# A retention mixer on one core: an item's split issued ahead of the next item's differences, and another order for the last gates and the last output rows

## The chip, the cores and the metric

One core of one Trainium2 chip runs the whole kernel in one launch. The metric is device time in microseconds (us). The median of 3 runs of the kernel before is 1352.68 (1351.59 to 1354.52). Engines are named as the profile names them: PE is the matrix engine (TensorE), PEld its weight loads, DVE the vector engine, ACT the scalar engine, POOL the GpSimd engine, SP the queue from which the DMAs start.

## The reference

Three layers follow each other, all in float32:

```
attention (8 batches, 8 heads, 576 rows, 64 columns):
    ret = (scale * q @ k.T) * decay(row - column);   x = ret @ v     -> 8 x 576 x 512
mixing:
    u = x + (x.T @ U @ V).T                          U, V of rank 32
    x2 = u + relu(u @ w_ch1) @ w_ch2                 512 -> 2048 -> 512
gated channel:
    xk, xr = mu * x2 + (1 - mu) * (x2 one row earlier)
    k = relu(xk @ w_k);  v = (k * k) @ w_v           512 -> 1024 -> 512
    out = sigmoid(xr @ w_r) * v
```

The rows of all batches together are 4608 columns of the kernel's tiles, which it treats as 9 blocks of 512. A float32 product is made of three matmuls: a value is split into a high part (a cast) and a low part (the value less the cast), and the products high × high, low × high and high × low are added in PSUM.

## The kernel before, in words

The whole kernel is under a manual schedule: each engine runs its instructions in the order in which the program issues them. Several large products are made by a scheme with seven products for a 2 × 2 block product, so that sums and differences of blocks are formed first.

Until 537 us the kernel does the attention, the mixing of low rank and `h = relu(u @ w_ch1)`. Then comes the stage around which the change stands, the second matrix of the mixing layer (`h @ w_ch2`) for blocks 0 to 7. It is cut into 64 **items**, in 4 quarters `q` of two halves `h` with 8 steps `j` each. An item of the first half (h = 0) gives four of the seven products (24 matmuls of 512 columns), one of the second half three (18 matmuls). Four groups of PSUM banks, `a` to `d`, two banks each, gather the products over the 8 steps.

The work of an item is spread over the engines. `load_item` (L464) loads its tiles `ra`, `rb` from memory, issued by SP. `sums_item` (L476) forms two differences on DVE: L480 and L481 in a first half, and SP stores the second of them for use in the second half; L484 and L485 in a second half. `split_item` (L487) makes for `ra` and then `rb` a cast on ACT (L499: `sah`, `sbh`) and a subtraction on DVE (L500: `sal`, `sbl`). `products` (L518) issues the matmuls (L540). At a half's last step `leave_group` (L550) takes the results out of the banks: copies on ACT (L554, L576), and for the products 4 and 3, at the quarter's end, additions on DVE that read banks `c` and `d` (L580). What is left to be done with them is put in a list, `rest`: additions on POOL (L557, L568, L571, L584, L590), an addition on DVE that reads banks `b` (L560), each final one with a small copy on ACT (L515) and a store by SP (L516). `load_rest` (L509) loads the tiles `ur` which they need.

The loop over items (L1372 to L1389) issues in iteration n: the loads of n+4, the differences of n+2, the split of n+1, the products of n, and then up to two entries of `rest`, except in a half's last step.

After the items, block 8 is projected (L620 to L622). Then, for each pair of blocks and last for block 8 alone in two sides of 256 columns, `gates` (L1423) makes the seven products for two column groups `g`, alternating between two sets of banks; `key_group` (L1465) makes the keys; and `value_part` (L1497) gathers the output products in four banks (L1507), multiplies them by the gate on DVE (L1517) and stores them (L1518). The matmuls of gates and keys are both at L1411; `load_keys` (L319) loads the key weights `wk` at L324.

Of the kernel before, what the change touches and what calls it, by code (L numbers as in the profile page):

```python
# [9 lines left out]
F32 = mybir.dt.float32  # L10
# [6 lines left out]
ALU = mybir.AluOpType  # L17
# [11 lines left out]
BT = 512  # L29
NB = T // BT  # L30
L = 64
NL = S // L
KD = DM // 128
# [7 lines left out]
def retention_mixer_kernel(ctx: ExitStack, tc: tile.TileContext, io):  # L41
    nc = tc.nc
# [14 lines left out]
    def unit(pool, dt, nm):  # L57
        return pool.tile([128, 2, 512], dt, tag="unit", name=nm)

    def small(dt, nm):  # L60
        return sm.tile([128, 512], dt, tag="small", name=nm)
# [179 lines left out]
    wv = [Weight(f"wv_{g}", io["moe2_w_v"][g * 512:(g + 1) * 512, :]) for g in range(2)]  # L241
# [5 lines left out]
    NG = DF2 // 256  # L247
# [209 lines left out]
    def col(p):  # L457
        return slice(p * 128, (p + 1) * 128)

    ITEMS = [(q, h, j) for q in range(NB // 2) for h in range(2) for j in range(NF // 2)]  # L460
# [3 lines left out]
    def load_item(n):  # L464
        q, h, j = ITEMS[n]
        ra[n] = unit(big2, F32, f"ra{n}")
        rb[n] = unit(big2, F32, f"rb{n}")
        if h == 0:
            nc.sync.dma_start(ra[n], hp[q][:, j, 0:2])
        else:  # L470
            nc.sync.dma_start(ra[n][:, 0], t1_blk[q][:, j])
        nc.sync.dma_start(rb[n], hp[q][:, j, 2:4])
# [3 lines left out]
    def sums_item(n):  # L476
        q, h, j = ITEMS[n]
        a, b = ra[n], rb[n]
        if h == 0:
            nc.vector.tensor_tensor(b[:, 0], b[:, 0], a[:, 1], op=ALU.subtract)  # L480
            nc.vector.tensor_tensor(a[:, 1], a[:, 1], a[:, 0], op=ALU.subtract)  # L481
            nc.sync.dma_start(t1_blk[q][:, j], a[:, 1])
        else:
            nc.vector.tensor_tensor(a[:, 0], b[:, 0], a[:, 0], op=ALU.subtract)  # L484
            nc.vector.tensor_tensor(b[:, 1], b[:, 1], a[:, 0], op=ALU.subtract)  # L485

    def split_item(n):  # L487
        q, h, j = ITEMS[n]
        a, b = ra.pop(n), rb.pop(n)
        x = {}  # L490
        two = (("a", a, big), ("b", b, big2))
        for nm, src, where in two[::-1] if h == 0 and j == 0 else two:
            hi = unit(big, F32R, f"s{nm}h{n}")
            lo = unit(where, F32R, f"s{nm}l{n}")
            if h == 1 and nm == "a":
                src, hi_, lo_ = src[:, 0], hi[:, 0], lo[:, 0]
            else:
                hi_, lo_ = hi, lo
            nc.scalar.copy(hi_, src)  # L499
            nc.vector.tensor_tensor(lo_, src, hi_.bitcast(F32), op=ALU.subtract)  # L500
            x[nm] = hi, lo
        parts_of[n] = x
# [6 lines left out]
    def load_rest(q, who):  # L509
        t, o = 2 * q + who % 2, who // 2  # L510
        ur[who] = unit(big2, F32, f"ur{t}_{o}")
        nc.sync.dma_start(ur[who], u_blk[t][:, 2 * o:2 * o + 2, :])
# [5 lines left out]
    def products(n):  # L518
        q, h, j = ITEMS[n]
        x = parts_of.pop(n)  # L520

        if h == 0:
            plan = {
                1: ("a", wp, 0, "a", 0), 2: ("b", wp, 1, "b", 1),
                5: ("d", wp, 2, "a", 1), 7: ("c", wp, 3, "b", 0),
            }
            seq_ = (2, 1, 7, 5) if j == 0 else (1, 7, 5, 2)
        else:
            plan = {6: ("a", wq, 2, "a", 0), 4: ("c", wq, 1, "b", 1), 3: ("d", wq, 3, "b", 0)}
            seq_ = (6, 4, 3)  # L530
        last = j == NF // 2 - 1
        for m in seq_:
            g, w, wi, nm, xi = plan[m]
            if h == 0 and j == 0:
                group[g] = [bank(2 * "abcd".index(g) + p, f"g{g}{q}_{p}") for p in range(2)]
            wh, wl = (v[:, wi] for v in w[j])
            xh, xl = (v[:, xi] for v in x[nm])
            for p in range(2):
                for i, (l, r) in enumerate(((wh, xh), (wl, xh), (wh, xl))):
                    nc.tensor.matmul(  # L540
                        group[g][p], l[:, col(p)], r,
                        start=(h == 0 and j == 0 and i == 0),
                        stop=(i == 2 and last),
                        skip_group_check=True,
                    )
            if last:
                for p in range(2):
                    leave_group(q, m, p, group[g][p])
# [48 lines left out]
    def load_hidden(p):  # L597
        hraw[p] = unit(big2, F32, f"hr{p}")
        nc.sync.dma_start(hraw[p], h_last[:, 2 * p:2 * p + 2, :])
# [3 lines left out]
    def split_hidden(p):  # L603
        r = hraw.pop(p)
        h, l = unit(big2, F32R, f"hh{p}"), unit(big2, F32R, f"hl{p}")
        nc.scalar.copy(h, r)
        nc.vector.tensor_tensor(l, r, h.bitcast(F32), op=ALU.subtract)
        hid[p] = h, l
# [133 lines left out]
    def columns(q):  # L742
        return BT if q < NB // 2 else BT // 2
# [7 lines left out]
    with ExitStack() as st:  # L751
# [375 lines left out]
        for i in range(WARM):  # L1127
# [4 lines left out]
                start=True,  # L1132
                stop=True,
# [238 lines left out]
    for n, (q, h, j) in enumerate(ITEMS):  # L1372
        if n + 4 < len(ITEMS):
            load_item(n + 4)
        if n + 2 < len(ITEMS):
            sums_item(n + 2)
        if n + 1 < len(ITEMS):
            split_item(n + 1)
        if j > 5:
            load_rest(q, ((0, 3), (2, 1))[h][j - 6])  # L1380
        if n >= len(ITEMS) - 4:
            load_hidden(n - len(ITEMS) + 4)
        if n == len(ITEMS) - 1:
            split_hidden(0)
        products(n)
        slot()
        for _ in range(2):
            if rest and j < NF // 2 - 1:
                rest.pop(0)()  # L1389

# [2 lines left out]
    gate, vacc, kk = {}, {}, {}  # L1393
    late = []

    def do_late():
# [3 lines left out]
    PLAN = {  # L1400
        1: ("a", 0, 0, "11"), 7: ("c", 0, 3, "t3"), 5: ("d", 0, 2, "t1"), 2: ("b", 0, 1, "21"),
        6: ("a", 1, 2, "t2"), 4: ("c", 1, 1, "t4"), 3: ("d", 1, 3, "22"),
    }
# [19 lines left out]
    def gates(q, bases, steps):  # L1423
        te, to = sides(q)
        n = columns(q)
        w = [(wrp.pop((q, g)), wrq.pop((q, g))) for g in range(2)]
        ps = [{}, {}]
        kept = {}

        def leave(t, o, x, y):  # L1430
            out = gate_of(t[0], o)[:, t[1]]
            nc.vector.tensor_tensor(out, x, y, op=ALU.add)
            nc.scalar.activation(out, out, AF.Sigmoid)

        for m, g in [(m, g) for m in PLAN for g in range(2)]:
            b = PLAN[m][0]
            if b not in ps[g]:
                ps[g][b] = bank(bases[g] + "abcd".index(b), f"r{b}{q}_{g}")[:, :n]
            x = product(m, w[g], xr, q, ps[g])
            if m in (1, 7, 5, 6):  # L1440
                kept[m, g] = small(F32, f"r{m}_{q}_{g}")[:, :n]
                nc.scalar.copy(kept[m, g], x)
            elif m == 2:
                leave(te, g, x, kept.pop((1, g)))
                y = kept.pop((5, g))
                nc.vector.tensor_tensor(kept[7, g], kept[7, g], y, op=ALU.add)
            elif m == 4:
                leave(te, g + 2, x, kept[6, g])
            else:
                leave(to, g, x, kept[6, g])  # L1450
                leave(to, g + 2, kept.pop((7, g)), kept.pop((6, g)))
            if g == 1:
                del xr[q, PLAN[m][3]]
                pump(steps)
# [42 lines left out]
    def value_part(t, g, base, more=0):  # L1497
        if g == 0:
            vacc[t] = [bank(base + o, f"v{t}_{o}") for o in range(KD)]
        do_late()  # L1500
        pump(more)
        kh, kl = kk.pop((t, g))
        for i in range(2):
            w = wv[i]
            for o in range(KD):
                for j, (lo, x) in enumerate(((0, kh), (1, kh), (0, kl))):
                    nc.tensor.matmul(  # L1507
                        vacc[t][o], w.part(lo, g, col(o)), x[:, i, :],
                        start=(g == 0 and i == 0 and j == 0),
                        stop=(g == NG - 1 and i == 1 and j == 2),  # L1510
                    )
            if g < NG - 1 or i == 0:
                pump(PUMP[0])
        if g == NG - 1:
            for o in range(KD):
                x = small(F32, f"o{t}_{o}")
                nc.vector.tensor_tensor(x, vacc[t][o], gate[t, o // 2][:, o % 2, :], op=ALU.mult)  # L1517
                nc.sync.dma_start(io["out"][col(o), t * BT:(t + 1) * BT], x)  # L1518
            pump(PUMP[0])

    PUMP = [0]
# [28 lines left out]
    for q in range(NB // 2 + 1):  # L1550
# [5 lines left out]
        if not last:  # L1556
            gates(q, (mine, other), 1 if q else 2)
            PUMP[0] = 2
            for g in range(NG):
                n = q * NG + g  # L1560
# [111 lines left out]
```

## Time and profile before

| | |
|---|---|
| median of 3 runs | 1352.68 us |
| profiled execution | 1349.82 us |
| its span on the core | 1348.0 us |
| PE busy | 1332.4 us, 99% |
| DVE busy | 845.5 us, 63% |
| ACT busy | 652.1 us, 48% |
| POOL busy | 337.4 us, 25% |
| granted PE clock, mean over the span | 0.995 |

Busy time is the time in which an engine's instructions ran. A timeline row has the start, the duration, the engine, the line of the kernel, the operation, the tiles written and read (numbers left out), the shapes, the count of instructions put together in the row, and in brackets the idle time ahead of it and what ended that. The profiled execution is one run, and rows are read on its own clock from the start of the span.

### The profile page before, as it was taken

What the parts mean: (1) busy time and instruction counts of PE and PEld (TensorE: products, weight loads), DVE (VectorE), ACT (ScalarE), POOL (GpSimd) and SP (SyncE); (2) the same over time, 40 slices, a digit from 0 to 9 for tenths busy, and PEclk for the clock granted to TensorE, in tenths of its full rate; (3) what the DMA queues carried; (4) which work ended last, traced back from release to release, by engine and by line L of the source; (5) the groups of instructions that cost most, each with busy time, mean ns of one, the idle gap of its engine ahead of it and who ended that gap; (6) DMA issues with size and microseconds to landing.
All of it is one profiled execution on the core that took longest, in us unless ns stands there. A gap on an engine that the chain in (4) does not pass through costs nothing.

```text
span 1348.0 us, 25775 instructions
## 1 busy us (share of the span) xinstructions
PE 1332.4 (99%) x10263; PEld 1096.0 (81%) x10263; DVE 845.5 (63%) x1173; ACT 652.1 (48%) x1133; POOL 337.4 (25%) x284
## 2 busy tenths in 40 slices
PE   7999999999999999999999999999999999999998
PEld 4778888888887888888888888888888888888897
DVE  4763333243340223989897987897787787787753
ACT  4664444434343466544444434565464464464431
POOL 2121232412222154023222112204204204204212
PEclk8899999999999999999999999999999999999999
DMA  8977698776653657969697886794174174273372
GB/s 292 333 260 247 210 334 286 273 275 242 215 209 149 211 198 256 318 234 313 196 308 274 296 277 223 261 334 185 65 272 163 70 271 160 71 273 124 111 282 77
DMA packets 124377, 308.26 MB, mean 229 GB/s; under 512 B 14496, under 2 KB 27040, under 8 KB 124256
## 3 DMA queue, kind: packets, MB, share of 16 engines
q1 hardware_dynamic: 124256, 306.60, 65.5%
q8 instruction: 81, 1.33, 0.4%
q14 instruction: 40, 0.33, 0.1%
HBM read 215.33 MB, written 91.23 MB: 227 GB/s over the span
## 4 chain that ended last, share of the span: by engine, by line
PE 93%; DVE 4%; DMA 1%; issue 1%; ACT 1%; SPq 0%; POOL 0%; DVEq 0%; ACTq 0%
PE h L368 29%; PE v L1507 14%; PE ga L540 6%; PE gc L540 6%; PE gd L540 5%; PE kc L1411 4%; PE kd L1411 4%; PE ka L1411 4%; PE gb L540 3%; PE kb L1411 2%; PE rd L1411 2%; PE rc L1411 2%; PE ra L1411 2%; PE xn L962 2%; PE up L854 1%; PE dn L876 1%
## 5 line engine op out<-in xcount | busy, mean ns | idle before, releaser
L374 ACT ACTIVATE hs<-h 128x512 f32<-128x512 f32 x144 | 86.0, 598 | 211.8 <-PE h L368 208.2
L1463 POOL TENSOR_TENSOR vl<-m,vh 128x512 fp32r<-128x512 f32 (+1 forms) x40 | 47.6, 1191 | 310.3 <-ACT vh L1462 240.0
L834 DVE TENSOR_TENSOR pm<-up,dtab 128x512 f32<-128x512 f32 (+1 forms) x40 | 25.4, 636 | 134.1 <-PE up L820 121.6
L499 ACT CAST sbh<-rb 128x1024 fp32r<-128x1024 f32 x64 | 67.3, 1052 | 59.9 <-PE gd L540 43.4
L500 DVE TENSOR_TENSOR sbl<-rb,sbh 128x1024 fp32r<-128x1024 f32 x64 | 85.3, 1333 | 7.8 <-ACT sbh L499 7.7
L1507 PE MATMUL v<-vh,wv_0u 128*128 128x512 f32 x288 | 88.8, 389 | 0.0
L1507 PE MATMUL v<-vh,wv_1u 128*128 128x512 f32 x288 | 88.7, 389 | 0.0
L500 DVE TENSOR_TENSOR sal<-ra,sah 128x1024 fp32r<-128x1024 f32 (+1 forms) x64 | 65.5, 1023 | 20.6 <-PE gd L540 12.7
L499 ACT CAST sah<-ra 128x1024 fp32r<-128x1024 f32 (+1 forms) x64 | 53.6, 837 | 50.7 <-DVE ra L481 19.6
L782 POOL TENSOR_TENSOR kv<-kv,ktab 128x512 f32<-128x512 f32 (+1 forms) x40 | 39.8, 995 | 142.7 <-DMA kv<-in_kv 101.0
L1463 POOL TENSOR_TENSOR vl<-c,vh 128x512 fp32r<-128x512 f32 (+1 forms) x40 | 62.2, 1574 | 25.8 <-ACT vh L1462 25.8
L1507 PEld LDWEIGHTS v<-vh,wv_1u 128*128 128x128 f32 x288 | 54.1, 188 | 11.2
L1507 PEld LDWEIGHTS v<-vh,wv_0u 128*128 128x128 f32 x288 | 53.9, 188 | 11.0
L1462 ACT CAST vh<-m 128x512 fp32r<-128x512 f32 (+1 forms) x40 | 23.2, 579 | 75.7 <-DVE m L1461 75.7
L1031 DVE TENSOR_TENSOR xt<-mx,xt 128x256 f32<-128x256 f32 x64 | 28.8, 457 | 49.2 <-PE mx L1027 49.0
L1507 PE MATMUL v<-vl,wv_0u 128*128 128x512 f32 x144 | 56.0, 389 | 0.0
L1507 PE MATMUL v<-vl,wv_1u 128*128 128x512 f32 x144 | 56.0, 389 | 0.0
L653 ACT ACTIVATE tp<-x2l,omu 128x511 f32<-128x511 f32 x72 | 50.9, 712 | 2.7 <-DMA x2l<-xb 1.4
L584 POOL TENSOR_TENSOR x<-x,ur 128x512 f32<-128x512 f32 x16 | 24.3, 1530 | 107.5 <-DMA ur<-ub 53.5
L557 POOL TENSOR_TENSOR m<-m,ur 128x512 f32<-128x512 f32 x8 | 12.2, 1557 | 133.6 <-ACT m L554 133.6
L1461 DVE SCALAR_TENSOR_TENSOR m<-m 128x512 f32<-128x512 f32 (+1 forms) x40 | 44.8, 1120 | 1.4
L1411 PE MATMUL kc<-kht,wk 128*128 128x512 f32 (+1 forms) x160 | 45.5, 368 | 0.0
(290 smaller groups left out, 3740.3 us busy)
## 6 DMA issues: line engine op xcount, KB each, us to landing
wk<-keys SPq DMA_DIRECT2D x80, 512.0 KB, 6.0
hp<-hs SPq DMA_DIRECT2D x128, 256.0 KB, 2.9
rb<-hp SPq DMA_DIRECT2D x64, 512.0 KB, 5.8
wr<-gates SPq DMA_DIRECT2D x40, 512.0 KB, 6.9
qk<-in_qk SPq DMA_DIRECT2D x32, 512.0 KB, 5.6
kv<-in_kv SPq DMA_DIRECT2D x32, 512.0 KB, 6.2
ra<-hp SPq DMA_DIRECT2D x32, 512.0 KB, 7.1
ur<-ub SPq DMA_DIRECT2D x18, 512.0 KB, 5.8
```

Source lines behind the costliest of these rows:

```text
L368: nc.tensor.matmul(hps[t, f], w.part(lo, k, fo), u[k // 2][:, k % 2, :], start=(part == 0 and k == 0), stop=(part == 2 and k == KD - 1),)
L374: nc.scalar.activation(h, hps.pop((t, f)), AF.Relu)
L499: nc.scalar.copy(hi_, src)
L500: nc.vector.tensor_tensor(lo_, src, hi_.bitcast(F32), op=ALU.subtract)
L540: nc.tensor.matmul(group[g][p], l[:, col(p)], r, start=(h == 0 and j == 0 and i == 0), stop=(i == 2 and last), skip_group_check=True,)
L653: nc.scalar.activation(tp[:, 1:], x[:, :BT - 1], AF.Copy, scale=omu[:, j, k:k + 1])
L782: nc.gpsimd.tensor_tensor(k, k, ktab[:, p, :n].to_broadcast([128, n, NP, D]), op=ALU.mult)
L1031: nc.vector.tensor_tensor(u, ps[:, :n], u, op=ALU.add)
L1411: nc.tensor.matmul(ps[b], l, r[:, i], start=(part == 0 and i == 0 and j == 0), stop=(i == 1 and j == 2), skip_group_check=True,)
L1461: nc.vector.scalar_tensor_tensor(x, x, 0.0, x, op0=ALU.max, op1=ALU.mult)
L1463: eng.tensor_tensor(l, x, h.bitcast(F32), op=ALU.subtract)
L1507: nc.tensor.matmul(vacc[t][o], w.part(lo, g, col(o)), x[:, i, :], start=(g == 0 and i == 0 and j == 0), stop=(g == NG - 1 and i == 1 and j ...
```

## The change

Four edits. In the item loop, the split of item n+1 is issued ahead of the differences of item n+2. In a half's first two steps, one entry of `rest` is taken in place of two. For the last gates (block 8), the order of the products is no longer (1,0), (1,1), (7,0), (7,1), ... but the set of banks 0 goes two products ahead: (1,0), (7,0), (1,1), (5,0), (7,1), (2,0), (5,1), (6,0), (2,1), (4,0), (6,1), (3,0), (4,1), (3,1). For the last block's last key group, `value_part` issues each output row's multiplication and store as soon as its products are issued, and makes the last row's (o = 3) in two halves of 256 columns, each with its own matmuls, multiplication and store.

```
     for n, (q, h, j) in enumerate(ITEMS):
         if n + 4 < len(ITEMS):
             load_item(n + 4)
+        if n + 1 < len(ITEMS):
+            split_item(n + 1)
         if n + 2 < len(ITEMS):
             sums_item(n + 2)
-        if n + 1 < len(ITEMS):
-            split_item(n + 1)
...
-        for _ in range(2):
+        for _ in range(1 if j < 2 else 2):
             if rest and j < NF // 2 - 1:
                 rest.pop(0)()
...
-        for m, g in [(m, g) for m in PLAN for g in range(2)]:
+        turns_of = [(m, 0) for m in PLAN], [(m, 1) for m in PLAN]
+        if q < NB // 2:
+            both = [x for pair in zip(*turns_of) for x in pair]
+        else:
+            both = turns_of[0][:1]
+            for x in zip(turns_of[0][1:], turns_of[1]):
+                both.extend(x)
+            both.append(turns_of[1][-1])
+        for m, g in both:
...
+        end = g == NG - 1
+
+        def block(i, o, cols=slice(None), whole=True):
+            w = wv[i]
+            for j, (lo, x) in enumerate(((0, kh), (1, kh), (0, kl))):
+                nc.tensor.matmul(
+                    vacc[t][o][:, cols], w.part(lo, g, col(o)), x[:, i, cols],
+                    start=(g == 0 and i == 0 and j == 0),
+                    stop=(end and i == 1 and j == 2), skip_group_check=(t == NB - 1 and o == KD - 1),
+                )
+
+        def exit_of(o, cols=slice(0, BT)):
+            n = cols.stop - cols.start
+            x = small(F32, f"o{t}_{o}")[:, :n]
+            nc.vector.tensor_tensor(x, vacc[t][o][:, cols], gate[t, o // 2][:, o % 2, cols], op=ALU.mult)
+            nc.sync.dma_start(io["out"][col(o), t * BT + cols.start:t * BT + cols.stop], x)
+
+        if end and t == NB - 1:
+            for i in range(2):
+                for o in range(KD - 1):
+                    block(i, o)
+                    if i:
+                        exit_of(o)
+            for n in range(2):
+                cols = slice(n * (BT // 2), (n + 1) * (BT // 2))
+                for i in range(2):
+                    block(i, KD - 1, cols, False)
+                exit_of(KD - 1, cols)
+            return
         for i in range(2):
...
             for o in range(KD):
...
+                block(i, o)
```

For all other blocks the matmuls, multiplications and stores of `value_part` are issued in the order of before.

## Rows read from the trace of the kernel before

**Rows 1.** Stretch of one quarter of items: start:end, us, busy us (x instructions), clock, DMA share, GB/s.

```profile
614.00:691.00 77.00, 76.86 (x338) 63.04 (x337) 66.88 (x71) 35.09 (x48) 20.07 (x13) 1.00 0.81 271
```

**Rows 2.** Timeline, first matmuls of the item stage and first behind it.

```profile
537.38 0.62 PE L540 MATMUL gb<-sbh,w2p 128*128 128x512 f32 x2
...
844.96 0.39 PE L620 MATMUL c<-hh,w2p 128*128 128x512 f32 x1
```

**Rows 3.** Waits in the item stage: engine, line, waited for: us in all, times, longest.

```profile
ACT edge L515 <- DVE m L560: 27.0, 8, 6.4
...
PEld ga L540 <- DVE sal L500: 3.1, 4, 1.1
```

**Rows 4.** Timeline, a round of DVE and ACT in a second half.

```profile
593.86 0.68 DVE L484 TENSOR_TENSOR ra<-rb,ra 128x512 f32<-128x512 f32 x1
...
594.58 0.69 DVE L485 TENSOR_TENSOR rb<-rb,ra 128x512 f32<-128x512 f32 x1
594.66 0.62 ACT L499 CAST sah<-ra 128x512 fp32r<-128x512 f32 x1 [0.60 <-DVE ra L484]
...
595.79 1.22 DVE L500 TENSOR_TENSOR sbl<-rb,sbh 128x1024 fp32r<-128x1024 f32 x1
```

**Rows 5.** Timeline, a round of DVE and ACT in a first half.

```profile
708.31 0.69 DVE L481 TENSOR_TENSOR ra<-ra 128x512 f32<-128x512 f32 x1
...
708.92 1.22 DVE L500 TENSOR_TENSOR sal<-ra,sah 128x1024 fp32r<-128x1024 f32 x1
...
709.17 1.06 ACT L499 CAST sah<-ra 128x1024 fp32r<-128x1024 f32 x1 [1.13 <-DVE ra L481]
...
710.06 1.22 DVE L500 TENSOR_TENSOR sbl<-rb,sbh 128x1024 fp32r<-128x1024 f32 x1
```

**Rows 6.** Timeline, the first item of a second half.

```profile
580.67 0.62 ACT L499 CAST sah<-ra 128x512 fp32r<-128x512 f32 x1
...
581.32 0.99 DVE L500 TENSOR_TENSOR sal<-ra,sah 128x512 fp32r<-128x512 f32 x1 [1.96 <-ACT sah L499]
581.35 0.39 PE L540 MATMUL ga<-sah,w2q 128*128 128x512 f32 x1
```

**Rows 7.** Timeline, DVE and POOL instructions that ran side by side.

```profile
616.73 2.32 DVE L500 TENSOR_TENSOR sal<-ra,sah 128x1024 fp32r<-128x1024 f32 x1
...
617.92 2.28 POOL L590 TENSOR_TENSOR m<-m,u 128x512 f32<-128x512 f32 x1
```

**Rows 8.** Timeline, the change from the first quarter to the second.

```profile
612.99 1.29 POOL L584 TENSOR_TENSOR x<-x,ur 128x512 f32<-128x512 f32 x1 [25.60 <-DVE x L580]
...
613.51 1.37 DVE L580 TENSOR_TENSOR x<-gd,u 128x512 f32<-128x512 f32 x2
...
613.99 0.39 PE L540 MATMUL gb<-sbh,w2p 128*128 128x512 f32 x1
```

**Rows 9.** Timeline of the last gates, and of a key matmul behind them.

```profile
1291.79 2.48 DVE L1517 TENSOR_TENSOR o<-v,g 128x512 f32<-128x512 f32 x4
...
1292.53 0.39 PE L1411 MATMUL ra<-rh,wr 128*128 128x256 f32 x1 [0.62 <-DVE o L1517]
...
1307.03 0.40 PE L1411 MATMUL ka<-kh,wk 128*128 128x256 f32 x2
```

**Rows 10.** Tile `wk`, the issue at 1297.7: line, queue, ns; then issue to landing.

```profile
L324 SPq DMA_DIRECT2D wk<-keys x1: 361/361/361, 1297.7 to 1297.7; - x1
...
DMA to landing us min/median/max: 9.2/9.2/9.2
```

**Rows 11.** Timeline, the last four multiplications.

```profile
1342.13 2.73 DVE L1517 TENSOR_TENSOR o<-v,g 128x512 f32<-128x512 f32 x4 [5.83 <-PE v L1507]
```

**Rows 12.** Tile `out`, the last four stores: line, queue, ns; then issue to landing.

```profile
L1518 SPq DMA_DIRECT2D out<-o x4: 332/334/338, 1342.9 to 1344.9; - x4
...
DMA to landing us min/median/max: 2.0/2.1/2.1
```

**Rows 13.** DMA issues of 128 KB: tiles, queue, KB, us to landing.

```profile
ub<-xt SPq DMA_DIRECT2D x2, 128.0 KB, 3.9
```

More of the change, by code (lines that the diff above doesn't have):

```diff
@@ L1502, in value_part @@
         kh, kl = kk.pop((t, g))
+        end = g == NG - 1
[24 more added lines that the diff above has]
+            return
         for i in range(2):
-            w = wv[i]
             for o in range(KD):
[L1506 to L1512, printed above, removed]
+                block(i, o)
+            if not end or i == 0:
                 pump(PUMP[0])
-        if g == NG - 1:
+        if end:
             for o in range(KD):
-                x = small(F32, f"o{t}_{o}")
-                nc.vector.tensor_tensor(x, vacc[t][o], gate[t, o // 2][:, o % 2, :], op=ALU.mult)
-                nc.sync.dma_start(io["out"][col(o), t * BT:(t + 1) * BT], x)
+                exit_of(o)
             pump(PUMP[0])
```

## Prediction

> **What bounds the kernel now.** I read the stages first. In the stretch of one quarter of the item stage TensorE is busy 76.86 us of 77.00 at a granted clock of 1.00 (the 2.4 GHz level), DVE 66.88, ACT 35.09, POOL 20.07 [rows 1]. So the end is set by TensorE's own work, 76.86 / 338 = 0.227 us a matmul of 512 columns, and another engine counts only where it makes TensorE wait. The stage's first and last rows give its length, 844.96 − 537.38 = 307.58 us [rows 2]; its 8 × (24 + 18) × 4 = 1344 matmuls take 304.8, which leaves some 2.7 us of stalls (2.73 is used below). The list of waits says where they are: TensorE's weight loads waited for `sal` (the low part from L500) four times, 3.1 us in all, 1.1 at most [rows 3]. That is one item per quarter. Everything that part 1 of the change can win is in those 2.7 us; DVE, with some 10 us free in 77, is the engine that can lose them many times over.
>
> **Part 1, the item's split ahead of the next one's differences.** No instruction is added or removed; DVE's order changes. Before, a round on DVE is differences of n+2 (L480, L481 or L484, L485), then `sal`, `sbl` of n+1. The casts of n+1 on ACT wait for differences that were made a round earlier, so they lie beside DVE's work. In a second-half round the cast `sah` runs from 594.66, just behind the end of L484 at 594.54, while DVE still goes through L485 [rows 4]; the four instructions follow without a gap, 593.86 to 597.01, about 3.1 us. A first-half round is 0.69 + 0.69 + 1.14 + 1.14 = 3.7 (starts 708.92 and 710.06 are 1.14 apart) [rows 5]. An item lasts 24 × 0.227 = 5.44 or 18 × 0.227 = 4.08 us, so DVE gains 1.7 or 1.0 us of lead (the time by which an item's splits are done before TensorE wants them) with each.
>
> After the change, DVE does the differences of n+1, and the very next thing it is to do is subtract the cast of them. It stands still for hand-over, cast and hand-back: the cast starts 0.12 to 0.17 after the difference (709.17 behind a difference that started at 708.31 and ended at 709.00) and takes 1.06 in a first half, 0.62 in a second [rows 4, 5]; the way back is 581.32 − (580.67 + 0.62) = 0.03 to some 0.09 [rows 6]. That is 1.27 or about 0.75 us a round. The second cast, 1.06, lies under the first subtraction. New rounds: 3.7 + 1.27 = 4.95 of 5.44, and 3.06 + 0.74 = 3.80 of 4.08. The steady state still holds, but the lead gained is 0.5 and 0.28 us an item in place of 1.7 and 1.0. Per quarter 8 × 1.27 + 8 × 0.74 = 16 us of waits come onto an engine that had 10 free.
>
> What spends the lead is beside the rounds. At a quarter's end four L580 (0.69 each, 2.75) read the banks `c` and `d`, and only then POOL has its block of six to eight additions; two L560 come in the second half. And a DVE subtraction beside a POOL addition goes from 1.22 to 2.32 us, the addition from 1.29 to 2.28 [rows 5, 7, 8].
>
> The chain at a change of quarter, with T the start of its first item (613.99 [rows 8]): at the middle of the quarter the lead is near nothing, since `sah` of item 8 is cast only behind ACT's bank copies (DVE waited 1.96 us there) and its `sal` starts 0.03 us before TensorE's first matmul of the item [rows 6]. Eight items give 8 × 0.28 = 2.2, the two L560 take 1.4: a lead of 0.8 where before it was some 4.5. Then:
> - The differences of the quarter's second item end at T + 2.5, and the L580 behind them run to T + 5.2 (before: 613.51 + 1.37 = T + 0.9 [rows 8]). TensorE wants the first bank `c` at T + 2.72 and gets it at T + 3.2: 0.5 us.
> - `sal` of the second item follows, 5.2 to 6.35 alone and to 7.5 beside POOL; it is wanted at 6.4: 1.1 us with POOL, nothing without.
> - `sbl` of it: 0.85, likewise.
> - The third item's differences, cast and `sal`: 1 to 2, I take 1.55.
>
> Sum 4.0 us a change of quarter. The ends: without any slowed pair 0.5, with every pair slowed in full and casts waiting 5.3. A second way, by amounts: from the end of the L580 to the need for the fourth item's `sal` there are 11.8 us; DVE has to do three `sal`, two `sbl` and two pairs of differences, 8.6, and POOL six additions of 1.28, 7.7. A pair that takes 2.32 and not 1.22 + 1.28 = 2.5 hides 7%, so (8.6 + 7.7) × 0.93 = 15.1: 3.3 too long, with the bank's 0.5 it is 3.8. I take 4.0, by the slowed rows, since POOL's additions wait for the same L580 (25.60 us, released by `x` of L580 [rows 8]) and so start with DVE's late work.
>
> The rule behind this stands in the Trainium skill, "SBUF — State Buffer", section "Who interferes with whom": a DVE instruction with two SBUF inputs contends with a GpSimd instruction that reads SBUF, for the port pair they share, and one with a single SBUF input does not. The trace agrees as far as it shows it: L580, with one input in PSUM, keeps 0.69 us beside POOL at 612.99 [rows 8]. Read as an exclusive lock, the 7% would go too, and the sum by amounts would be an estimate of 16.3 − 11.8 + 0.5 = 5.0 and not 3.8.
>
> Three changes of quarter: 3 × 4.0 = 12.0. The stalls of before are in that chain and are not counted twice: −2.73.
>
> **Part 2, one pop less for j < 2.** It issues the same instructions later; POOL takes them as their inputs arrive, so its work is not spread. What moves is ACT's edge copy (L515): the two L560 now come with item 10, each edge copy waits for its L560 and stands in ACT's queue ahead of the cast of item 12. ACT waited 27.0 us in 8 of these before, 6.4 at most, under cover of a lead [rows 3]. Without one it costs 0 to 0.9; I take 0.4, four times: +1.6. On SP the `ur` loads (L512) now stand behind a store of differences (L482) that come a round later; POOL gets them later, which is inside the bounds above. Item stage: 12.0 + 1.6 − 2.73 = +10.9.
>
> **Part 3, order of the last gates.** Matmuls, banks and instructions are the same; the set of bank bases that DVE's last `o` must free is wanted one product later. TensorE waited 0.62 us, its load 0.82, for the L1517 that ended at 1292.43 [rows 9]; with the new order one more product of set 0, 6 matmuls of half 0.227, 0.7 us, stands ahead of it: most of the 0.8 would go, at most 0.9 with a second, smaller wait. But the next limit is near: the key weight issued at 1297.7 lands 9.2 later, at 1306.9 [rows 10], and its matmul started at 1307.03 [rows 9]. If TensorE comes 0.9 earlier it finds the weight late by 0.6. I take −0.3 (0 to −0.9).
>
> **Part 4, the last rows.** The same columns go through TensorE, 12 matmuls of 256 in place of 6 of 512; two of 256 are 0.40 from first start to last end, one of 512 0.39 [rows 6, 9]: 6 × 0.01 = +0.06. Before, four L1517 run 1342.13 to 1344.86 and the last store is issued at once [rows 11], landing 2.1 us later [rows 12]. After it, the last multiply is on 256 columns, some 0.3 shorter. The smaller store: 128 KB took 3.9 us elsewhere, and this 256 KB took 2.1 [rows 12, 13]: between no gain and a loss covered by the first half's; I take none. −0.25 (0 to −0.6).
>
> **Sum.** +10.9 − 0.3 − 0.25 = +10.3. The profiled execution took 1349.82 (span 1348.0 and 1.8 around it), so 1360.1; the median of the runs lies 2.86 above it: 1363.0.
>
> **Rivals.**
> - A, faster: the lead is enough and `sal` comes sooner because it no longer stands behind the next differences. Then the 2.73 go, with parts 3 and 4 −3.3: 1349.4. For it: both new rounds are shorter than their items, and the four stalls are waits for `sal`, which is what the order moves ahead. Against: the casts are exposed just where L580 and POOL come. It decides if the lead at the quarter's end is over 3 us.
> - B, about even: POOL does its additions while DVE waits for casts, so pairs hardly meet. Then 0.5 a change of quarter: 1.5 + 1.6 − 2.73 − 0.55 = −0.2, with half of the slowing +1 to +3; 1350 to 1356, middle 1353. For it: 16 us of cast waits against 20 of POOL. Against: POOL runs its block in one piece.
> - C, the likeliest, slower: as summed. Its ends are 2.5 and 5.3 a change of quarter: 3 × 2.5 − 2.73 − 0.55 + 0 = +4.2, and 15.9 + 1.6 − 2.73 = +14.8: 1357 to 1367.5.
>
> **How the numbers follow.** C 0.74, A 0.15, B 0.11. The range, 1350.5 to 1367.5, takes in B and C and leaves out most of A; C's own is 1357 to 1367. About 0.2%, 2.7 us, is what can be told from no change, so A is faster, B falls on same by two thirds with the rest to both sides: faster 0.16, same 0.08, slower 0.76.
>
> **What would show it.** Right: DVE idle before each `sal`, released by `sah`, about 1.3 and 0.75 us, 64 times; TensorE waits on `sal`, `sbl` and bank `c` in the first three items of quarters 2 to 4, 4 us each; L580 ending some 5 us into the item. In the last gates no wait on L1517, and one on the key weight instead. Last: two stores of `out` for the last rows. Wrong: if L500 beside POOL stays near 1.2 us, or the item stage lasts less than 309 us, the lead was enough and C falls. If TensorE's stalls are at items 10 to 13 instead, part 2 was mis-sized.

## The result, and the profile after

The changed kernel takes 1365.12 us (median of 6 runs, 1364.83 to 1366.17), the kernel before 1352.72 on the same chip (6 runs). The ratio is 1.0092, 95% interval 1.008 to 1.0105: slower, by 12.4 us. 1363.0 was forecast, in a range of 1350.5 to 1367.5.

The profiled execution of the changed kernel has a span of 1363.1 us, 15.1 more than before. Four stretches of the timeline make it up: the item stage begins 1.46 later (the program up to there is the same, see the last section), lasts 13.35 longer, TensorE takes 0.82 more from there to its last matmul, and the end behind that is 0.53 shorter.

The item stage, from the timeline (against [rows 2]):

```profile
538.84 0.62 PE L540 MATMUL gb<-sbh,w2p 128*128 128x512 f32 x2
...
859.77 0.39 PE L620 MATMUL c<-hh,w2p 128*128 128x512 f32 x1
```

859.77 − 538.84 = 320.93 us, 307.58 before. One quarter, from its first item to the next quarter's (columns as in [rows 1]):

```profile
615.54:696.54 81.00, 78.40 (x338) 62.38 (x337) 66.98 (x71) 33.93 (x49) 19.71 (x12) 1.00 0.80 260
```

The quarter of the same work lasts 81.0 us, not 77; DVE's busy time is what it was (66.98 against 66.88), so it is not more work. TensorE's weight loads now wait in this stage as follows (engine, line, waited for: us in all, times, longest; against [rows 3]):

```profile
PEld ga L540 <- DVE sal L500: 10.5, 13, 2.0
PEld ga L540 <- ACT sah L499: 4.9, 7, 1.1
PEld gc L540 <- DVE sbl L500: 4.3, 8, 1.0
PEld gc L540 <- DVE x L580: 0.6, 3, 0.2
```

The four waits for `sal`, 3.1 us, have become 13 of 10.5, and others have come beside them, 31 of 20.3 us in all. A weight load waits while earlier matmuls still run, so TensorE itself lost less: 320.93 − 304.64 = 16.3 us, where 304.64 is the time of its 1344 matmuls. The place of each is found by taking the starts of an item's first matmul and the next item's, less 24 or 18 matmuls of 0.2267 us. That gives 5.7 us near the middle of the quarters (items 12, 26 to 28, 42 to 44, 58 to 60) and 10.5 at the changes of quarter (16 to 19, 32 to 34 and 35, 49 and 50).

The change of quarter in the timeline of the changed kernel (against [rows 8], T = 615.54 in place of 613.99), DVE and POOL, then TensorE's first stall:

```profile
616.15 0.68 DVE L480 TENSOR_TENSOR rb<-rb,ra 128x512 f32<-128x512 f32 x1
616.87 0.69 DVE L481 TENSOR_TENSOR ra<-ra 128x512 f32<-128x512 f32 x1
617.48 1.28 DVE L580 TENSOR_TENSOR x<-gc,u 128x512 f32<-128x512 f32 x2
618.43 2.55 POOL L584 TENSOR_TENSOR x<-x,ur 128x512 f32<-128x512 f32 x2 [28.45 <-DVE x L580]
618.67 1.28 DVE L580 TENSOR_TENSOR x<-gd,u 128x512 f32<-128x512 f32 x2
619.87 2.20 DVE L500 TENSOR_TENSOR sal<-ra,sah 128x1024 fp32r<-128x1024 f32 x1
...
622.12 0.50 PE L540 MATMUL ga<-sal,w2p 128*128 128x512 f32 x1 [0.42 <-DVE sal L500]
```

The L580 end at 619.95, T + 4.4 (T + 0.9 before). POOL's addition runs beside the `sal` that TensorE wants next, which takes 2.20 and not 1.2. Two items further on, a difference is slowed as well, so the cast behind it is late, and TensorE waits for the cast itself:

```profile
629.19 1.77 DVE L480 TENSOR_TENSOR rb<-rb,ra 128x512 f32<-128x512 f32 x1
630.37 1.74 POOL L590 TENSOR_TENSOR m<-m,u 128x512 f32<-128x512 f32 x1
631.00 1.66 DVE L481 TENSOR_TENSOR ra<-ra 128x512 f32<-128x512 f32 x1
632.74 1.05 ACT L499 CAST sah<-ra 128x1024 fp32r<-128x1024 f32 x1 [5.96 <-PE gd L540]
633.84 0.73 PE L540 MATMUL ga<-sah,w2p 128*128 128x512 f32 x2 [0.60 <-ACT sah L499]
```

ACT's 5.96 idle is put down to a matmul (L540) that was done earlier, but the cast starts 0.08 after L481's end (631.00 + 1.66). The middle of the same quarter, where POOL's other block (L557, L568, L571) runs:

```profile
662.36 1.74 POOL L557 TENSOR_TENSOR m<-m,ur 128x512 f32<-128x512 f32 x1
664.06 1.29 POOL L568 TENSOR_TENSOR m<-m,m 128x512 f32<-128x512 f32 x1
664.14 2.29 DVE L500 TENSOR_TENSOR sbl<-rb,sbh 128x1024 fp32r<-128x1024 f32 x1 [1.18 <-POOL m L557]
665.43 2.15 POOL L571 TENSOR_TENSOR m<-m,ur 128x512 f32<-128x512 f32 x1
666.35 1.78 DVE L484 TENSOR_TENSOR ra<-rb,ra 128x512 f32<-128x512 f32 x1
668.16 1.66 DVE L485 TENSOR_TENSOR rb<-rb,ra 128x512 f32<-128x512 f32 x1
669.75 1.78 DVE L500 TENSOR_TENSOR sal<-ra,sah 128x512 fp32r<-128x512 f32 x1
671.58 0.50 PE L540 MATMUL ga<-sal,w2q 128*128 128x512 f32 x1 [0.83 <-DVE sal L500]
```

Four DVE instructions in a row are slowed, the last of them the `sal` that TensorE waits for in item 26; and the first of them had stood still for 1.18 us until POOL's L557 was done, which is a wait and not a slowing. Two items later the edge copies stand ahead of a cast:

```profile
677.62 1.28 DVE L560 TENSOR_TENSOR m<-gb,m 128x512 f32<-128x512 f32 x2
678.93 0.19 ACT L515 COPY edge<-m 128x1 f32<-128x1 f32 x1 [0.41 <-DVE m L560]
679.03 0.61 ACT L499 CAST sah<-ra 128x512 fp32r<-128x512 f32 x1
679.68 0.69 DVE L500 TENSOR_TENSOR sal<-ra,sah 128x512 fp32r<-128x512 f32 x1 [0.78 <-ACT sah L499]
```

The differences for that cast were done at 677.70; it waits for the second L560 and its copy until 679.03.

The last gates and the last row: the waits of the weight loads from 1300 us on, and the end of the timeline (against [rows 9, 11]):

```profile
PEld v L1516 <- DVE o L1525: 0.7, 1, 0.7
PEld ka L1411 <- DMA wk<-keys: 0.5, 1, 0.5
```

```profile
1356.13 2.49 DVE L1525 TENSOR_TENSOR o<-v,g 128x512 f32<-128x512 f32 x4 [5.15 <-PE v L1516]
...
1358.68 0.51 PE L1516 MATMUL v<-vh,wv_0u 128*128 128x256 f32 x2 [0.52 <-DVE o L1525]
...
1359.76 0.42 DVE L1525 TENSOR_TENSOR o<-v,g 128x256 f32<-128x256 f32 x1 [1.14 <-PE v L1516]
```

In the gates the bank is hardly waited for any more, the key weight is. And at the end there is a wait that was not forecast: the second half of the last row starts only when DVE has multiplied the first half (1356.13 + 2.49 = 1358.62); 1358.68 − 1357.88, less the 0.115 of a matmul, is 0.68 us, and 0.11 more go with the next one.

### The profile page after: what moved, and what is told of

Its sections match the earlier page's. It is cut to its first block, busy times and chain, and to the rows that moved or that the text cites. A ratio compares the mean times of both kernels' runs of the same rounds, so it can differ in the third digit from the quotient of the medians.

```text
span 1363.1 us, 25823 instructions
## 1 busy us (share of the span) xinstructions
PE 1338.4 (98%) x10269; PEld 1094.2 (80%) x10269; DVE 850.0 (62%) x1174; ACT 648.5 (48%) x1133; POOL 338.2 (25%) x284
## 3 DMA queue, kind: packets, MB, share of 16 engines
q8 instruction: 81, 1.33, 0.4%
## 4 chain that ended last, share of the span: by engine, by line
PE 84%; DVE 6%; issue 3%; DMA 3%; ACT 3%; SPq 0%; POOL 0%; ACTq 0%; DVEq 0%
PE h L368 29%; PE v L1516 14%; PE ka L1411 4%; PE kd L1411 4%; PE kc L1411 4%; PE gd L540 3%; PE gc L540 3%; PE ga L540 3%; PE gb L540 2%; PE ra L1411 2%; PE kb L1411 2%; PE rd L1411 2%; PE rc L1411 2%; PE xn L962 2%; ACT sbh L499 2%
## 5 line engine op out<-in xcount | busy, mean ns | idle before, releaser
L500 DVE TENSOR_TENSOR sal<-ra,sah 128x1024 fp32r<-128x1024 f32 (+1 forms) x64 | 70.5, 1102 | 35.9 <-ACT sah L499 35.0
L1516 PE MATMUL v<-vl,wv_0u 128*128 128x512 f32 (+1 forms) x145 | 56.2, 388 | 0.0
L1516 PE MATMUL v<-vl,wv_1u 128*128 128x512 f32 (+1 forms) x145 | 56.2, 387 | 0.0
L557 POOL TENSOR_TENSOR m<-m,ur 128x512 f32<-128x512 f32 x8 | 11.3, 1438 | 135.1 <-DMA rb<-hp 74.4
```

Of the source, the lines that this page charges most:

```text
L1516: nc.tensor.matmul(vacc[t][o][:, cols], w.part(lo, g, col(o)), x[:, i, cols], start=(g == 0 and i == 0 and j == 0), stop=(end and i == 1 a ...
```

## The experiments

Stage and stalls are from each run's profile, stalls worked out as above, all in us. The ratio is to the kernel before on the same chip, estimated from all runs of both, so it differs by about 0.001 at most from the quotient of the medians. That kernel's median was 1352.72 beside the changed one, 1352.58 beside the four parts alone, 1352.74 beside the changed kernel without POOL's additions, the one with the `rb` parts first and the two with four items, and 1351.89 beside the last four rows. "Middle" and "changes" are items 10 to 12, 26 to 28 and so on, and 16 to 19, 32 to 35, 48 to 51.

| kernel | stage | first items | middle | changes | median us | ratio (95%) |
|---|---|---|---|---|---|---|
| before | 307.58 | 0.45 | 0 | 2.49 | | |
| changed | 320.93 | 0 | 5.70 | 10.51 | 1365.12 | 1.0092 (1.008 to 1.0105) |
| order alone | 322.31 | 0 | 6.84 | 10.81 | 1370.11 | 1.0120 (1.0099 to 1.0140) |
| pops alone | 308.49 | 0.45 | 0 | 3.40 | 1353.59 | 1.0003 (0.9988 to 1.0018) |
| gates alone | 307.75 | 0.45 | 0 | 2.66 | 1353.16 | 1.0001 (0.9987 to 1.0014) |
| tail alone | 307.51 | 0.49 | 0 | 2.39 | 1354.46 | 1.0003 (0.9987 to 1.0018) |
| changed, no POOL additions | 304.64 | 0 | 0 | 0 | 1349.46 | 0.9982 (0.9969 to 0.9995) |
| changed, `rb` parts first | 317.70 | 0 | 4.57 | 8.32 | 1361.86 | 1.0074 (1.0057 to 1.009) |
| ahead at four items | 305.32 | 0.68 | 0 | 0 | 1350.75 | 0.9988 (0.9977 to 0.9998) |
| the same, gates, mended tail | 305.31 | 0.67 | 0 | 0 | 1348.84 | 0.9975 (0.9966 to 0.9985) |
| changed without part 2 | 321.69 | 0 | 7.98 | 9.06 | 1366.93 | 1.0107 (1.0093 to 1.0121) |
| changed again | 321.17 | 0 | 5.10 | 11.29 | 1365.54 | 1.0100 (1.0087 to 1.0114) |
| before, no POOL additions | 305.09 | 0.45 | 0 | 0 | 1351.59 | 0.9995 (0.9983 to 1.0007) |
| ahead until there is lead | 304.88 | 0 | 0 | 0.24 | 1349.45 | 0.9977 (0.9966 to 0.9989) |

1344 matmuls of 0.2267 are 304.64, so this is the stage without any stall.

**The four parts, one at a time.**

```diff
+        if n + 1 < len(ITEMS):
+            split_item(n + 1)
         if n + 2 < len(ITEMS):
             sums_item(n + 2)
-        if n + 1 < len(ITEMS):
-            split_item(n + 1)
```

> The kernel before with part 1 alone (an item's split ahead of the next one's differences). Theory: the order alone makes nearly all of the loss. The item stage, 307.6 us before and 320.9 in the changed kernel, is then 319 to 321, with TensorE's stalls in items 17 to 19, 33 to 35 and 49 to 51 (about 3.4 us a change of quarter) and some 1 us more near the tenth to twelfth item of a quarter; the time 1363 to 1366. Rival 1, that the later pops of the list make the stalls of items 26, 28, 42, 44, 58 and 60 (5.6 us together): the stage is 315, the time 1360. Rival 2, that order and pops are harmful only together: stage below 311, time below 1356.

The stage was 322.31, above the theory's 319 to 321, and the time 1370.11, 4 us above its range; both rivals fall. The order alone makes the whole loss of the stage, and the stalls of the middle are there without the later pops.

```diff
-        for _ in range(2):
+        for _ in range(1 if j < 2 else 2):
             if rest and j < NF // 2 - 1:
```

> The kernel before with part 2 alone (one pop less in a half's first two steps). Theory: with the old order the lead covers the later pops, so the item stage stays within 0.5 us of 307.6 and the time within 2 us of the kernel before. Rival: the additions on banks b and the edge copies, an item later, stand ahead of a cast that is wanted: +3 to +6 us, with stalls at items 12, 28, 44 and 60.

No stall at items 12, 28, 44 or 60; the stage is 0.9 longer, at item 18 (1.56 us), a little more than expected. In the old order the pops cost next to nothing.

```diff
-        for m, g in [(m, g) for m in PLAN for g in range(2)]:
+        turns_of = [(m, 0) for m in PLAN], [(m, 1) for m in PLAN]
...
+        for m, g in both:
```

> The kernel before with part 3 alone (order of the last gates). Theory: TensorE's stall of 0.89 us for the bank shrinks to about 0.17 and a wait of about 0.6 for the key weight takes its place: 0.1 us gained, time as before. Rival: the key weight comes early enough in this schedule and 0.7 to 0.9 us are gained. The trace tells them apart, the median does not.

The bank's 0.89 us became 0.17, the key weight's wait was 0.40 in this run: 0.3 gained, between the two. With the old gates the key weight's wait was nothing in the kernel before, 0.36 in the tail-alone run and 0.9 in the pops-alone run (the weight load's wait), so this landing moves by up to 0.9 us between runs, and what part 3 gains moves with it.

```diff
+            for n in range(2):
+                cols = slice(n * (BT // 2), (n + 1) * (BT // 2))
+                for i in range(2):
+                    block(i, KD - 1, cols, False)
+                exit_of(KD - 1, cols)
```

> The kernel before with part 4 alone (last output rows, the last one in two halves). Theory from the trace of the changed kernel: the second half's first matmul waits about 0.8 us for DVE's multiplication of the first half; the end behind the last matmul is 0.35 shorter; net +0.4 to +0.6 us from the last key matmul to the end. Rival, the step as predicted: no such wait, net -0.25.

The same wait as in the changed kernel, here in the timeline of this run:

```profile
1346.77 0.28 PE L1508 MATMUL v<-vl,wv_1u 128*128 128x256 f32 x1
1347.57 0.50 PE L1508 MATMUL v<-vh,wv_0u 128*128 128x256 f32 x2 [0.52 <-DVE o L1517]
```

0.79 in all. From the last key matmul's start to the last output matmul's start it is 11.75 us in place of 10.80, and from there to the end 3.77 in place of 4.21: net +0.52, as the theory had it (+0.42 in the changed kernel).

**Without POOL's additions.** In each of the five places of `rest` the addition is replaced by nothing:

```diff
-                nc.gpsimd.tensor_tensor(x, x, ur[who][:, p], op=ALU.add)
+                pass
```

> The changed kernel without the additions that POOL makes in the item stage (L557, L568, L571, L584, L590 are left out, so the rows that they feed lack those terms; loads, copies and stores stay). Theory: the exposed casts only use up the lead, and it is DVE's slowing beside POOL that then turns into stalls; without POOL the new rounds of 4.95 and 3.80 us fit their items and the stage falls from 320.9 to 305 to 307 us. Rival: the exposed casts and the four L580 are enough by themselves; the stage stays above 314.

304.64 us: no stall is left, which is just below the theory's range. The list of waits of TensorE's weight loads in the stage is empty. DVE at the same change of quarter:

```profile
618.03 1.28 DVE L580 TENSOR_TENSOR x<-gd,u 128x512 f32<-128x512 f32 x2
619.22 1.21 DVE L500 TENSOR_TENSOR sal<-ra,sah 128x1024 fp32r<-128x1024 f32 x1
...
624.15 1.23 DVE L500 TENSOR_TENSOR sal<-ra,sah 128x1024 fp32r<-128x1024 f32 x1 [1.25 <-ACT sah L499]
```

The exposed cast is still there, 1.25 us, but DVE keeps its lead: the L580 end at 619.31, 1.5 us behind the quarter's first matmul (617.79), and not 4.4; and `sal` takes 1.21, not 2.20. So the new rounds do fit, and only together with POOL's additions do they stall TensorE.

Without the additions the stores and edge copies behind them start sooner too, so this run by itself doesn't show by which of their effects they do harm. Item 26 tells them apart. Its `sal`, and the matmul that wants it, in this run:

```profile
664.83 0.69 DVE L500 TENSOR_TENSOR sal<-ra,sah 128x512 fp32r<-128x512 f32 x1
...
669.92 0.39 PE L540 MATMUL ga<-sal,w2q 128*128 128x512 f32 x1
```

It is done 4.40 us ahead. In the changed kernel nothing of that was left and TensorE stalled for 1.13, so DVE lost 5.5 us on the way, although the cast of item 25 ended 4.13 us before its use in both. The four slowed instructions shown for the changed kernel took 4.2 us more than alone, the `sal` of item 25 ahead of them 0.3 more, and the wait for L557 was 1.18. At this place, then, DVE's slowing beside POOL is about four fifths of the loss, and the wait for POOL's result the rest. That wait comes twice in this profile of the changed kernel, and not in the other one; there the items 26 and 42 stalled for 0.61 and 0.72, here for 1.13 and 1.33.

The counterpart, the same edit on the kernel before:

> The kernel before without POOL's additions in the item stage (left out; loads, copies and stores stay). Theory: the stalls of items 17, 18, 34 and 50 come from DVE's slowing beside POOL and go, that of item 1 (no additions yet) stays: stage 304.6 to 305.2. Rival: they come from the four L580 ahead of the split, and at least 1.5 us of them stays: stage above 306.3.

Only item 1's stall stays, 0.45. The stalls of before at items 17, 18, 34 and 50 had the same cause; the rival, the four L580 by themselves, falls.

**The `rb` parts first.**

```diff
-        for nm, src, where in two[::-1] if h == 0 and j == 0 else two:
+        for nm, src, where in two[::-1] if h == 0 else two:
...
-            seq_ = (2, 1, 7, 5) if j == 0 else (1, 7, 5, 2)
+            seq_ = (2, 1, 7, 5) if j == 0 else (1, 7, 5, 2) if last_ else (2, 7, 1, 5)
```

> The changed kernel, but in first-half items the parts of rb are split ahead of those of ra (its difference L480 is the first of the two, so its cast runs beside L481), and TensorE takes the products of rb first in steps 1 to 6. DVE's wait for a cast falls from about 1.27 to 0.5 us an item, nothing else gets less. Theory: exposed casts are what took the lead, so 0.75 us an item comes back: about 2.2 us less a change of quarter and no stall at items 26, 42 and 58; the stage is 309 to 314 us (320.9 in the changed kernel). Rival: what stalls is the block of L580 and POOL additions whatever the lead is; the stage stays above 318.

317.70: neither, though close to the rival. 3.2 us came back, not 7 to 12. The expectation counted on eight items of a first half saving lead for the second; this run's timeline shows that they can't:

```profile
656.46 1.05 ACT L499 CAST sbh<-rb 128x1024 fp32r<-128x1024 f32 x1 [2.58 <-PE gd L541]
657.42 1.17 ACT L555 COPY m<-ga 128x512 f32<-128x512 f32 x2
657.54 1.22 DVE L500 TENSOR_TENSOR sbl<-rb,sbh 128x1024 fp32r<-128x1024 f32 x1 [2.94 <-ACT sbh L499]
...
661.21 0.62 ACT L499 CAST sah<-ra 128x512 fp32r<-128x512 f32 x1
```

At the end of the first half more lead can't be used: DVE waits 2.94 us for a cast that itself waits until TensorE is done with a tile. Then six bank copies stand ahead of the cast for the tenth item of the quarter (item 25), which starts at 661.21 here and at 661.30 in the changed kernel. It ends 4.14 us before TensorE wants it here, and 4.13 there, in the kernel before and in the run without POOL's additions. What is saved before that point is lost there.

**An early split only where one is late.**

```diff
+    AHEAD = {0, 17, 33, 49}
...
+        if n + 1 < len(ITEMS) and n in AHEAD:
+            split_item(n + 1)
         if n + 2 < len(ITEMS):
             sums_item(n + 2)
-        if n + 1 < len(ITEMS):
+        if n + 1 < len(ITEMS) and n not in AHEAD:
             split_item(n + 1)
```

> The kernel before, with the split ahead of the next differences in four iterations only (n = 0, 17, 33 and 49, ahead of the items 1, 18, 34 and 50 that stalled). The item's own differences then lie an iteration further back, so that its cast is not exposed. Theory: an earlier split does help where it is late and costs nothing there: the stalls of these items (0.45 + 0.45 + 0.97 + 0.82 us) go, the stage falls from 307.6 to 305 to 305.6 us, the time by about 2.3 us. Rival: the differences that are put back come late for the next item, stalls move to items 2, 19, 35 and 51, and the stage stays at 307 or more.

305.32, in the range. All stalls at the changes are gone; the one of item 1 moved to item 2 (0.68), as the rival had it for that place alone. DVE also makes four sums of weights there (L421 to L424, 0.42 us each); that they are the reason was not tested. So part 1's idea is sound at three items, and the order is harmful as a rule for all.

**The best version.** The same with part 3, and part 4 with this end:

```diff
+            for i in range(2):
+                block(i, KD - 1, half[0], False)
+            exit_of(KD - 1, half[0])
+            block(1, KD - 2)
+            exit_of(KD - 2)
+            for i in range(2):
+                block(i, KD - 1, half[1], False)
+            exit_of(KD - 1, half[1])
```

> The same four iterations, with part 3 (order of the last gates) and part 4 mended: the last row's first half stands ahead of the third row's last products, so that DVE's multiplication of it is done before TensorE comes to the second half. Expected: stage 305 to 305.6; last gates 0.1 to 0.5 better; no wait at the second half, 0.4 better behind the last matmul; together 2.5 to 3.3 us under the kernel before. Rival: the multiplication of the first half still holds up the second, and the end is as long as with part 4 as it was (+0.4).

1348.84 us against 1352.74, ratio 0.9975 (0.9966 to 0.9985): faster than both kernels. Of the 3.9 us between the medians (2.5 to 3.3 were expected) the profile accounts for 2.7: the stage gave 2.27 and the gates 0.64, and the end took 0.18 more. So the mended end isn't the 0.4 better that was expected: from the last key matmul to the end it takes 15.19 us, against 15.43 with part 4 as it was and 15.01 before. The second half still waits a little, 0.16, since the first half's multiplication stands behind two others on DVE:

```profile
1339.11 1.89 DVE L1528 TENSOR_TENSOR o<-v,g 128x512 f32<-128x512 f32 x3 [5.04 <-PE v L1519]
...
1341.05 0.50 PE L1519 MATMUL v<-vh,wv_0u 128*128 128x256 f32 x2
```

With the split ahead in the first six iterations too (`AHEAD = {0, 1, 2, 3, 4, 5, 17, 33, 49}`):

> As the version with the four iterations, mended gates and end, but ahead in the first six iterations (n = 0 to 5), then at 17, 33 and 49. In those first items no addition runs on POOL, so the exposed cast is paid from DVE's free time, and the lead at the sixth item, 3 us in the changed kernel, covers the differences put back there. Expected: the 0.67 us at item 2 go, stage 304.6 to 304.8, the time 0.4 to 0.8 lower than that version, some 4 us under the kernel before. Rival: the stall moves on to item 7 or 8 and nothing is gained.

The stall of item 2 went, 0.24 came at item 49: stage 304.88, just above its range. The time, 1349.45 (ratio 0.9977), can't be told from the version before it.

**Part 2 in the new order.** The changed kernel with two entries of the list in every step, beside the changed kernel itself:

> The changed kernel with part 2 alone undone (two entries of the list in every step), beside the changed kernel itself on the same chip. As predicted before the change, part 2 costs 1.6 us, so without it the stage would be 319.3 and the time 1.6 lower. The runs so far (order alone 322.3, with all parts 320.9) speak for the other sign: stage 322 to 323, time 1 to 2 us above the changed kernel. If the time is 4 us or more above it, something outside the item stage is in it too.

> The changed kernel once more, as the partner of the one without part 2: stage 320.5 to 321.5, time 1364.5 to 1366.5.

The stage without part 2 is 321.69 (322 to 323 was expected), with it 321.17 and 320.93; order alone, the same item stage as without part 2, had 322.31. Part 2 gains 0.5 to 1.4 us in the stage, where a loss of 1.6 was forecast; since two profiles of one item stage differ by 0.2 and 0.6, the sign is likely and the size is not told. The times, 1366.93 (1365.22 to 1367.65) and 1365.54 (1364.20 to 1367.74), overlap. The 5 us between order alone and the changed kernel are not all explained by this; 2.7 of the 4.2 between their spans lie ahead of the stage.

## Why the prediction was right, and where not

- *DVE's order exposes the cast, the steady state holds.* Right for a first half, only in part for a second. In a first half DVE waits 1.25 us for `sah` (1.27 forecast), and a round takes 4.94 (L480 starts at 636.09 and, for the next item, at 641.03; 4.95 forecast). In a second half the wait is not ahead of `sal`: its cast lies beside L485, and DVE waits 0.44 ahead of `sbl` instead. The round is 3.72, not 3.80. So not 64 waits for `sah`: within the stage there are 30 of `sal` for `sah`, 35.0 us, and 28 of `sbl` for `sbh`, 11.4.
- *The chain at a change of quarter, 4.0 us each.* Right in kind: 2.9, 3.7 and 3.9, 10.5 in all for 12.0. Of its terms, bank `c` cost 0.1 and not 0.5, since the L580 ended at T + 4.4 and not at T + 5.2; `sbl` of the second item cost nothing in the first change; the third and fourth items together cost 1.9 to 2.3, where 1.55 was put down for the third. The second way, by amounts with the slowed pair, gave 3.8 and came nearest. The rule of the Trainium skill that was weighed there, "SBUF — State Buffer", section "Who interferes with whom", is borne out by the run without additions: the same `sal` takes 1.21 without POOL beside it, 2.20 with it, and two L580 take 1.28 in both. The sum with a full lock (5.0) was too high, but that doesn't speak against the lock: instruction by instruction the rows are a full block less 0.14 us (last section). With the measured end of the L580, T + 4.4, the same sum gives 16.3 − 12.6 + 0.1 = 3.8.
- *The lead at the middle of a quarter is near nothing.* Wrong, by a misread row. The `sal` that starts at 581.32 in [rows 6] is not item 8's but item 9's: the split of item 8 is issued ahead of the bank copies, that of item 9 behind them. In the kernel before, `sal` of item 8 and the first matmul that wants the one of 581.32 are these:

```profile
574.59 0.69 DVE L500 TENSOR_TENSOR sal<-ra,sah 128x512 fp32r<-128x512 f32 x1 [1.64 <-PE gd L540]
...
585.88 0.39 PE L540 MATMUL ga<-sal,w2q 128*128 128x512 f32 x1
```

So the lead there is 585.88 − 582.31 = 3.6 us, and in the changed kernel it is the same (`sal` of item 25 is done 3.6 us ahead, that of item 24 4.4). What the step missed is that POOL's other block, in the first items of a second half, spends this lead, and that the edge copies then meet none: 5.7 us of stalls at the middle, 2.1 of them for the edge copies, where 1.6 was counted, and that under part 2. The lead of 0.8 at the quarter's end, on which the chain rests, came out near the 1.1 measured for `sal` of item 16 by luck: it started 3.6 too low and left POOL's block out.
- *Part 2, +1.6.* Wrong in sign. The edge copies ahead of a cast do cost about 0.5 us each, but they do so with either count of pops, at items 11, 27, 43, 59 or one later. They belong to part 1.
- *Part 3, −0.3.* Right: −0.3 alone, −0.1 in the changed kernel, −0.6 in the best version, depending on when the key weight lands, which is the next limit, as said.
- *Part 4, −0.25.* Wrong in sign: the end behind the last matmul gained 0.4 to 0.5, but between the two halves, which share a bank, TensorE waited 0.79 for DVE. (Whether halves in different banks would be free of it was not run.) The sum of the step's own terms had no place for a wait inside the last row.
- *Sum.* +10.3 forecast, +12.4 measured. The stage gave +13.35 for +10.9: the changes 1.5 less, the middle 4.1 more. Two errors of opposite sign made the total better than its terms; that much of the agreement is luck.
- *Rival A* (the lead is enough): this is what happens without POOL's additions, and with them at the three items where the differences are already made. *Rival B* fails, since POOL's block and DVE's late work start on the same event.

## What to carry to other kernels

A consumer put straight behind its producer on one engine with a cast on another in between costs a whole round trip each time; leave the work of the next item between them, and break that order only at the item that is late. Before moving work to where an engine still has room on average, list which blocks of an engine that slows it start on the same event, for all places of the period and not only the worst one. When a last tile is cut in two so that its parts overlap, put other matmuls between the parts (0.16 us of wait was left here, of 0.79); the whole end still gained nothing by it here.

## What the runs showed of the hardware that was not expected

- The same program up to the item stage reached it between 537.38 and 542.22 us in the 14 profiles; the differences are there within the first 100 us (the 1500th matmul came at 86.5 to 91.4 us), and are then carried along. What makes them was not followed up. These 4.8 us compare with 7.5 between the fastest and the slowest run of the kernel before (1348.8 to 1356.3 us) and are larger than three of the four parts of the change, so those were read from stretches of the trace and not from medians.
- A DVE instruction with both inputs in SBUF that starts while a POOL addition runs ends as if it had stood still until POOL is done and then taken its whole own time, less 0.14 us: L481 at 631.00 ended at 632.66, POOL's L590 beside it at 632.11, and 632.11 + 0.69 − 0.14 = 632.66. This holds for the 35 such meetings in the item stage of the kernel before and the 36 in the changed one, within 0.11 to 0.14 us. So 0.69 became up to 1.79 and 1.22 up to 2.32 us, by how much of POOL's instruction was left; what looked like 7% hidden in a pair is this constant. With one input in PSUM DVE kept 0.69.
